# Layer-norm statistics one pair earlier, key-value sums taken tile by tile, num and den in separate PSUM banks: a linear-attention and Mish layer on one core

## The chip, the core and the metric

The kernel runs on one core of a Trainium2 chip. The metric is the device time of one execution in microseconds (us). The engines are TensorE (PE, its weight loads PEld), VectorE (DVE), ScalarE (ACT), GpSimd (POOL) and SyncE (SP). Each works through its own stream of instructions in order and waits for the others at semaphores.

## The reference, cut to what matters

`x` is 2048 x 448 in bf16. The result is `x` plus two branches that both read the layer norm of `x`: linear attention with 16 heads of 28, and a feed-forward part of width 1792 with Mish.

```python
xn = layernorm(x)                                   # per row, eps 1e-5
q, k, v = split_heads(xn @ wqkv)                    # H = 16, Dh = 28
phi_q = concat(softmax(q @ w_phi), softmax(-(q @ w_phi)))    # per head
phi_k = concat(softmax(k @ w_phi), softmax(-(k @ w_phi)))
kv, z = phi_k^T v, sum over s of phi_k              # per head, over all 2048 rows
A = ((phi_q kv) / (phi_q z + 1e-6)) @ wo
h = xn @ w1 + b1
B = (h * tanh(softplus(h))) @ w2
out = x + A + B
```

`kv` and `z` need all 2048 rows before any row of `A` can be finished. The feed-forward part needs only `xn`.

## The kernel before, in words

The 2048 rows are 16 tiles of 128; two tiles are a pair, so there are 8 pairs (`NP`). Everything stays in SBUF. `Prog.add` (L53) appends each operation to its engine's stream in the order of the Python code, and works out the semaphore waits from three lists of names: what it reads (`r`), writes (`w`) and which of the eight PSUM banks it uses (`x`). Any two engines that use the same bank are ordered. No planner reorders anything: the order of the code is the order on each engine.

**The loop over the pairs** (L491) is the first stage. `ln_a(j)` (L471) takes the statistics of a pair: two `bn_stats` (L251) and two `bn_aggr` (L254) on VectorE, then on GpSimd an add (L257) and a power of minus one half (L259) for `rstd`. `ln_b(j)` (L478) normalises its two tiles on VectorE (L263). `xT` transposes them on TensorE (L298) and ScalarE copies them out (L301). `vproj` (L310), `kproj` (L320) and, one pair behind, `qproj` (L347; a quarter of the rows and half of the heads each time) are 8 matmuls each. VectorE copies v out (`vevac`, L467), ScalarE takes both exponentials of k (`kexp`, L327, into a ring of four `Ek`) and of q (`qexp`, L354). Two pairs behind, `knorm` makes the softmax of k: a sum on VectorE (`Sk`, L333), its reciprocal (`rSk`, L335), and on GpSimd the multiplication that writes `phik` (L336). `masks()` (L239) puts five small operations on GpSimd in iteration 2. In iteration j the order is: `ln_a(j+2)`, `xT(j+1)`, `vproj(j)`, `vevac(j)`, `ln_b(j+2)`, `kproj(j)`, `kexp(j)`, `qproj` and `qexp` of j-1, `knorm(j-2)`. So on GpSimd `rstd` of pair j+2 stands behind the multiplication of `knorm(j-3)`, and on VectorE `ln_b(j+2)` stands ahead of the sum of `knorm(j-2)`.

**The up-projection** (L522) has 28 groups n: 8 matmuls (`ffn1_mm`, L418) into two of the banks 0 to 3, and one Mish on ScalarE (L432). Behind group 6 `kvz` (L358) runs 128 matmuls (L363) that sum `kv` and `z` over all tiles into banks 6 and 7, and VectorE masks them into `KVZ` (L370, L374). From group 7 on each group carries one row tile m: num and den by `nd_mm` (L381, four matmuls each for s = 1 into bank 7 and for s = 0 into bank 6), the division on VectorE (`nd`, L386, five operations L389 to L397) and GpSimd (L398), and three tiles behind the transposition of the attention rows (`oTr`, L405) in bank 4.

**The down-projection** (L536) gives every row tile 14 matmuls with W2 (L441) and 4 with Wo (L446) in one accumulation, an add of x on VectorE (L451) and a store.

Of the kernel before, what the change touches and what calls it, by code (L numbers as in the profile page):

```python
# [146 lines left out]
def ap_on(src, dims):  # L147
    return bass.AP(tensor=src.tensor, offset=src.offset, ap=[list(src.ap[0])] + [list(d) for d in dims])
# [9 lines left out]
def _kernel(es, nc, x2, A_wqkv, A_w_phi, A_wo, B_w1, B_b1, B_w2, out2):  # L158
    KC, KP, QG = 4, 112, 4
    E1 = DH + 1  # L160
    E2 = DH + 2
    pr = Prog(nc, es)
    pe = lambda fn, **k: pr.add("PE", fn, **k)
# [7 lines left out]
    def sb(name, shape, dtype=BF16):  # L171
        return es.enter_context(nc.sbuf_tensor(name, shape, dtype))
# [3 lines left out]
    mask = sb("mask", [KP, QG, E1], FP32)  # L176
# [25 lines left out]
    phik = hm[1].rearrange("p a b -> p (a b)").rearrange("p (t f) -> p t f", t=NT)  # L202
    rq = [sb(f"rq{i}", [P, 2, H], FP32) for i in range(2)]
    t1 = [sb(f"t1_{i}", [P, H, E1], FP32) for i in range(2)]
    t2 = [sb(f"t2_{i}", [P, H, E1], FP32) for i in range(2)]
# [5 lines left out]
    PS = es.enter_context(nc.psum_tensor("PS", [P, 8, 512], FP32))  # L211
# [38 lines left out]
    def ln_stats(t):  # L250
        dve(lambda v: v.bn_stats(stats[:, t, :], x_all[:, t, :]), r=[f"x{t}"], w=[f"st{t}"])  # L251

    def ln_aggr(t):
        dve(lambda v: v.bn_aggr(mv[:, t, :], stats[:, t, :]), r=[f"st{t}"], w=[f"mv{t}"])  # L254
# [7 lines left out]
    def ln_norm(t, eng):  # L262
        eng(lambda v: v.tensor_scalar(xn[t % NXN][:, :], x_all[:, t, :], mv[:, t, 0:1], rstd[:, t:t + 1],  # L263
                                      op0=ALU.subtract, op1=ALU.mult),
            r=[f"x{t}", f"mv{t}", f"rs{t}"], w=[f"xn{t % NXN}"])
# [76 lines left out]
    def qproj(tc, gp):  # L342
        for u in range(2):
            g = 2 * gp + u
            def f(e, g=g, u=u):
                for c in range(KC):
                    i = e.matmul(PS[0:KP, 6 + u, :], Wp[:, 0, c, g * KP:(g + 1) * KP],  # L347
                                 xnT[:, c, tc * 512:(tc + 1) * 512], start=(c == 0), stop=(c == KC - 1))
                return i
            pe(f, r=[f"xT{2 * tc}", f"xT{2 * tc + 1}", "Wp0"], x=[6 + u])  # L350

    def qexp(tc, gp):
        for s in range(2):
            act(lambda a, s=s: a.activation(EqT[:, s, 2 * gp:2 * gp + 2, tc * 512:(tc + 1) * 512],  # L354
                                            PS[0:KP, 6:8, :], ACT.Exp, scale=(1.0 if s == 0 else -1.0)),
                w=[f"Eq{tc}{gp}{s}"], x=[6, 7])

    def kvz():  # L358
        for s in range(2):
            def f(e, s=s):  # L360
                for g in range(QG):
                    for t in range(NT):
                        i = e.matmul(PS[0:KP, 6 + s, g * QG * E1:(g + 1) * QG * E1],  # L363
                                     phik[:, t, s * D + g * KP:s * D + (g + 1) * KP],
                                     v_ext[:, t, 4 * g:4 * g + 4, :], start=(t == 0), stop=(t == NT - 1))
                return i
            pe(f, r=[f"phik{j}" for j in range(8)] + [f"v{j}" for j in range(8)] + ["v1"], x=[6 + s])
            mk = ap_on(mask[:, 0, 0:1], [[0, QG], [E1, QG], [1, E1]])
            ps = PS[0:KP, 6 + s, 0:QG * QG * E1].rearrange("p (g j c) -> p g j c", g=QG, j=QG)
            dve(lambda v, s=s, mk=mk, ps=ps: v.tensor_tensor(KVZ[:, s, :, :, 0:E1], ps, mk, ALU.mult),  # L370
                r=["mask"], w=[f"KVZa{s}"], x=[6 + s])
            if s == 0:
                mz = ap_on(mask[:, 0, DH:E1], [[0, QG], [E1, QG], [1, 1]])
                dve(lambda v, mz=mz, ps=ps: v.scalar_tensor_tensor(KVZ[:, 0, :, :, DH:E1], ps[:, :, :, DH:E1],  # L374
                                                                   DEN_EPS, mz, op0=ALU.add, op1=ALU.mult),
                    r=["mask"], w=["KVZa0"], x=[6])

    def nd_mm(t, s):
            def f(e):
                for g in range(QG):  # L380
                    i = e.matmul(PS[:, 6 + s, g * QG * E2:(g + 1) * QG * E2], EqT[:, s, g, t * P:(t + 1) * P],  # L381
                                 KVZ[:, s, g, :, :], start=True, stop=True)
                return i
            pe(f, r=[f"Eq{t // 4}{gp}{s}" for gp in range(2)] + [f"KVZa{s}", "KVZ1"], x=[6 + s])

    def nd(t):  # L386
        i = t % 2
        nds = [PS[:, 6 + s, 0:H * E2].rearrange("p (h c) -> p h c", c=E2) for s in range(2)]
        dve(lambda v: v.reciprocal(rq[i][:, 1, :], nds[1][:, :, E1]), w=[f"rq{i}"], x=[7])  # L389
        dve(lambda v: v.tensor_tensor(rq[i][:, 0, :], nds[0][:, :, E1], rq[i][:, 1, :], ALU.mult),  # L390
            r=[f"rq{i}"], w=[f"rho{i}"], x=[6])
        dve(lambda v: v.tensor_tensor(t2[i][:, :, :], nds[1][:, :, 0:E1],  # L392
                                      ap_on(rq[i][:, 0, 0:1], [[1, H], [0, E1]]), ALU.mult),
            r=[f"rho{i}"], w=[f"t2{i}"], x=[7])
        dve(lambda v: v.tensor_tensor(t1[i][:, :, :], nds[0][:, :, 0:E1], t2[i][:, :, :], ALU.add),
            r=[f"t2{i}"], w=[f"t1{i}"], x=[6])
        dve(lambda v: v.reciprocal(rden[i][:, :], t1[i][:, :, DH]), r=[f"t1{i}"], w=[f"rd{i}"])  # L397
        pool(lambda g: g.tensor_tensor(o_sb[t % NO][:, :].rearrange("p (h d) -> p h d", d=DH), t1[i][:, :, 0:DH],  # L398
                                       ap_on(rden[i][:, 0:1], [[1, H], [0, DH]]), ALU.mult),
             r=[f"t1{i}", f"rd{i}"], w=[f"o{t % NO}"])  # L400
# [11 lines left out]
    def ffn1_mm(n, u):  # L412
        tcp, fc = n // FC, n % FC
        b = 2 * (n % 2)
        def f(e):
            for c in range(KC):
                o = tcp * 1024 + u * 512
                i = e.matmul(PS[:, b + u, :], W1[:, c, fc * P:(fc + 1) * P], xnT[:, c, o:o + 512],  # L418
                             start=(c == 0), stop=(c == KC - 1))
            return i  # L420
        pe(f, r=["W1"] + [f"xT{4 * tcp + 2 * u}", f"xT{4 * tcp + 2 * u + 1}"], x=[b + u])

    def mish(n):
        tcp, fc = n // FC, n % FC
        b = 2 * (n % 2)
        if tcp:
            rr = [f"phik{j}" for j in range(8)]
        elif fc < 7:
            rr = [f"WT{w}{h}" for w in range(2) for h in range(2)]
        else:  # L430
            rr = [f"Ek{i}{u}" for i in range(4) for u in range(2)]
        act(lambda a: a.activation(hm[tcp][:, fc, :].rearrange("p (u n) -> p u n", u=2), PS[:, b:b + 2, :], ACT.Mish,  # L432
                                   bias=b1T[:, fc:fc + 1]), r=["b1T"], w=[f"hm{tcp}"] + rr, x=[b, b + 1])
# [21 lines left out]
    NP = NT // 2  # L455
# [32 lines left out]
    w_mm(1, 0)  # L488
    w_mm(1, 1)
    ln_b(1)  # L490
    for j in range(NP):  # L491
        if j + 2 < NP:
            ln_a(j + 2)
        if j + 1 < NP:
            xT(j + 1)
        vproj(j)
        vevac(j)
        if j + 2 < NP:
            ln_b(j + 2)
        if j == 0:  # L500
            w_trans(0, 0)
            w_trans(0, 1)
        kproj(j)
        kexp(j)
        if j == 0:
            w_mm(0, 0)
            w_mm(0, 1)
        if j >= 1:
            qproj((j - 1) // 2, (j - 1) % 2)
            qexp((j - 1) // 2, (j - 1) % 2)  # L510
        if j >= 2:
            knorm(j - 2)
        if j == 2:
            masks()
            pe(lambda e: e.transpose(PSb[:, 3, 0:FC], b1_rows[0:FC, :], ident[0:FC, 0:FC]), r=["b1r", "ident"], x=[3])
            dve(lambda v: v.tensor_copy(b1T[:], PSb[:, 3, 0:FC]), w=["b1T"], x=[3])
    qproj(3, 1)
    qexp(3, 1)
    knorm(NP - 2)
    knorm(NP - 1)  # L520
    KV_AT = 6
    for n in range(2 * FC):  # L522
        m = n - KV_AT - 1
        ffn1_mm(n, 0)
        if 0 <= m < NT:
            nd_mm(m, 1)
        ffn1_mm(n, 1)
        mish(n)
        if 0 <= m < NT:
            nd_mm(m, 0)  # L530
            nd(m)
        if n == KV_AT:
            kvz()
        if 0 <= m - 3 < NT:
            oTr(m - 3)
# [31 lines left out]
```

## Time and profile before

| what | value |
|---|---|
| median of 3 runs | 201.37 us (201.27 to 204.5) |
| the profiled execution | 200.96 us, of which the traced span 199.0 us |
| mean granted TensorE clock | 0.983 |
| TensorE matmul busy | 176.7 us, 89% |
| VectorE busy | 84.4 us, 42% |
| ScalarE busy | 85.4 us, 43% |
| GpSimd busy | 51.7 us, 26% |

The span runs from the first to the last instruction; the remaining 1.96 us of the profiled execution lie around it. The matmul share is an average over stages, and matmuls waiting in the pipe count as busy. The stages are to be read one by one: the loop over pairs ends at about 67 us of the span, the up-projection runs to 141.57 us, and the down-projection fills the rest.

### The profile page before, as it was taken

How to read it: one execution, taken by the hardware profiler on the slowest of the kernel's cores; microseconds unless marked ns; L12 is line 12 of the kernel's file. 1: busy time of each engine (PE TensorE's matmuls, PEld its weight loads, DVE VectorE, ACT ScalarE, POOL GpSimd, SP SyncE). 2: the span in 40 equal slices, each digit the busy share in tenths (PEclk: the TensorE clock that was granted, in tenths of full speed). 3: DMA queues.
4: the chain of work that ended last, by engine and by line, in shares of the span. 5: the costliest groups of instructions: out<-in, count | busy, mean ns of one | idle time of the engine just before them, and what ended most of it. 6: DMA issues, size and time to landing. Idle time of an engine off the chain costs nothing.

```text
span 199.0 us, 2766 instructions
## 1 busy us (share of the span) xinstructions
PE 176.7 (89%) x1153; PEld 97.9 (49%) x1153; DVE 84.4 (42%) x172; ACT 85.4 (43%) x94; POOL 51.7 (26%) x54
## 2 busy tenths in 40 slices
PE   0579599959959598999999999999999999999994
PEld 0455455434535243487455555554455555555551
DVE  1535057565968950003777777770021211212121
ACT  2553768854767738640456666678500000000000
POOL 3310110838439795000233333331000000000000
PEclk9999999979999969999999999999999999999999
DMA  6999900000000000000000000000001010100101
GB/s 161 296 320 292 276 1 0 0 3 2 0 0 0 0 0 3 2 0 3 0 0 3 0 0 3 0 2 3 0 23 46 23 49 23 41 28 23 49 23 46
DMA packets 7556, 8.69 MB, mean 44 GB/s; under 512 B 952, under 2 KB 6840, under 8 KB 7544
## 3 DMA queue, kind: packets, MB, share of 16 engines
q1 hardware_dynamic: 6544, 8.09, 13.8%
q10 hardware_dynamic: 968, 0.43, 0.8%
q8 instruction: 9, 0.15, 0.3%
q14 instruction: 3, 0.02, 0.0%
q0 software_dynamic: 32, 0.00, 0.0%
HBM read 6.68 MB, written 1.84 MB: 43 GB/s over the span
## 4 chain that ended last, share of the span: by engine, by line
PE 72%; POOL 7%; DVE 7%; ACT 6%; DMA 4%; issue 1%; ACTq 0%; DVEq 0%; POOLq 0%
PE PS L418 21%; PE PS L441 21%; PE PS L446 6%; POOL hm L336 5%; PE PS L310 5%; PE PS L381 4%; DMA Wbd<-in_A_w_phi_dram 4%; PE PS L347 4%; PE PS L363 3%; PE PS L320 3%; DVE Sk L333 3%; ACT EqT L354 2%; PE PS L405 2%; ACT hm L327 2%; PE PS L284 1%; PE PS L298 1%
## 5 line engine op out<-in xcount | busy, mean ns | idle before, releaser
L418 PE MATMUL PS<-xnT,W 112*128 112x512 bf16 x224 | 54.7, 379 | 0.9 <-ACT hm L432 0.9
L441 PE MATMUL PS<-W,hm 128*128 128x448 bf16 x224 | 45.0, 353 | 0.0
L432 ACT ACTIVATE hm<-PS,b1T 128x1024 bf16<-128x1024 f32 x28 | 31.2, 1114 | 27.7 <-PE PS L418 27.6
L451 DVE TENSOR_TENSOR out_sb<-PS,x_all 128x448 bf16<-128x448 f32 x16 | 10.0, 625 | 53.0 <-PE PS L446 53.0
L441 PEld LDWEIGHTS PS<-W,hm 128*128 128x128 bf16 x224 | 21.9, 98 | 20.6
L336 POOL TENSOR_TENSOR hm<-hm,rSk 128x1792 bf16<-128x1792 bf16 x8 | 25.6, 3209 | 16.9 <-DVE rSk L335 11.5
L418 PEld LDWEIGHTS PS<-xnT,W 112*128 112x128 bf16 x224 | 20.3, 98 | 19.5 <-ACT hm L432 1.4
L327 ACT ACTIVATE hm<-PS 128x896 bf16<-128x896 f32 x16 | 13.8, 914 | 12.0 <-PE PS L320 12.0
L347 PE MATMUL PS<-xnT,Wp 112*112 112x512 bf16 x64 | 16.8, 410 | 2.0 <-ACT EqT L354 2.0
L354 ACT ACTIVATE EqT<-PS 112x1024 bf16<-112x1024 f32 x16 | 15.5, 1021 | 3.7 <-PE PS L347 3.7
L310 PE MATMUL PS<-Wqkv,xnT 112*128 112x448 bf16 x64 | 16.3, 407 | 0.0
L333 DVE TENSOR_REDUCE Sk<-hm 128x64 f32<-128x1792 bf16 x8 | 16.0, 2000 | 0.0
L398 POOL TENSOR_TENSOR o_sb<-t_0,rden 128x448 bf16<-128x448 f32 x8 | 7.5, 941 | 30.3 <-DVE rden L397 30.3
L446 PE MATMUL PS<-Wo,EqT 112*128 112x448 bf16 x64 | 14.8, 352 | 0.0
L467 DVE CAST v_ext<-PS 128x896 bf16<-128x896 f32 x8 | 8.6, 1078 | 14.0 <-PE PS L310 14.0
L320 PE MATMUL PS<-Wp,xnT 112*128 112x448 bf16 x64 | 13.5, 353 | 0.4 <-ACT hm L277 0.4
L381 PEld LDWEIGHTS PS<-KVZ,EqT 112*128 112x128 bf16 x128 | 8.3, 98 | 11.0 <-DVE t_0 L392 3.8
L347 PEld LDWEIGHTS PS<-xnT,Wp 112*112 112x112 bf16 x64 | 8.7, 138 | 8.4 <-ACT EqT L354 2.5
L381 PE MATMUL PS<-KVZ,EqT 112*128 112x120 bf16 x128 | 12.1, 217 | 0.5 <-DVE t_1 L392 0.2
L251 DVE BATCH_NORM_STATS2 stats<-x_all 128x6 f32<-128x448 bf16 x16 | 9.1, 608 | 4.2 <-DMA x_all<-in_A_x_dram 4.2
L298 PE MATMUL PS<-ident,xn 128*112 128x128 bf16 x64 | 6.5, 257 | 4.8 <-DVE xn L263 4.8
L398 POOL TENSOR_TENSOR o_sb<-t_1,rden 128x448 bf16<-128x448 f32 x8 | 7.5, 941 | 12.2 <-DVE rden L397 12.2
(49 smaller groups left out, 146.1 us busy)
## 6 DMA issues: line engine op xcount, KB each, us to landing
W<-in_B_w_dram SPq DMA_DIRECT2D x2, 1568.0 KB, 17.4
out_dram<-out_sb SPq DMA_DIRECT2D x16, 112.0 KB, 1.7
x_all<-in_A_x_dram SPq DMA_DIRECT2D x1, 896.0 KB, 10.0
Wqkv<-in_A_wqkv_dram SPq DMA_DIRECT2D x2, 392.0 KB, 7.3
x_all<-in_A_x_dram SPq DMA_DIRECT2D x2, 224.0 KB, 4.3
x_all<-in_A_x_dram SPq DMA_DIRECT2D x1, 448.0 KB, 7.1
Wqkv<-in_A_wqkv_dram ACTq DMA_DIRECT2D x1, 392.0 KB, 4.9
Wo<-in_A_wo_dram SPq DMA_DIRECT2D x1, 392.0 KB, 21.2
```

The costliest lines, as they stand in the source:

```text
L310: i = e.matmul(PS[:, 2 + u, 0:D], xnT[:, c, t * P:(t + 1) * P], Wqkv[:, c, 2 * D:3 * D], start=(c == 0), stop=(c == KC - 1))
L320: i = e.matmul(PS[:, 4 + u, 0:D], xnT[:, c, t * P:(t + 1) * P], Wp[:, 1, c, :], start=(c == 0), stop=(c == KC - 1))
L327: act(lambda a, s=s: a.activation(Ek[j % 4][:, :, s, :], PS[:, 4:6, 0:D], ACT.Exp, scale=(1.0 if s == 0 else -1.0)), w=[f"Ek{j % 4}{s}"], ...
L333: dve(lambda v: v.tensor_reduce(Sk[b][:, :], Ek[q][:, :, :, :].rearrange("p t s (h f) -> p (t s h) f", f=DH), AX.X, ALU.add), r=[f"Ek{q}0" ...
L336: pool(lambda g: g.tensor_tensor(phik[:, 2 * j:2 * j + 2, :].rearrange("p t (k f) -> p (t k) f", f=DH), Ek[q][:, :, :, :].rearrange("p t s ...
L347: i = e.matmul(PS[0:KP, 6 + u, :], Wp[:, 0, c, g * KP:(g + 1) * KP], xnT[:, c, tc * 512:(tc + 1) * 512], start=(c == 0), stop=(c == KC - 1))
L354: act(lambda a, s=s: a.activation(EqT[:, s, 2 * gp:2 * gp + 2, tc * 512:(tc + 1) * 512], PS[0:KP, 6:8, :], ACT.Exp, scale=(1.0 if s == 0 e ...
L381: i = e.matmul(PS[:, 6 + s, g * QG * E2:(g + 1) * QG * E2], EqT[:, s, g, t * P:(t + 1) * P], KVZ[:, s, g, :, :], start=True, stop=True)
L418: i = e.matmul(PS[:, b + u, :], W1[:, c, fc * P:(fc + 1) * P], xnT[:, c, o:o + 512], start=(c == 0), stop=(c == KC - 1))
L432: act(lambda a: a.activation(hm[tcp][:, fc, :].rearrange("p (u n) -> p u n", u=2), PS[:, b:b + 2, :], ACT.Mish, bias=b1T[:, fc:fc + 1]), r ...
L441: i = e.matmul(PS[:, b, 0:D], hm[t // 8][:, fc, o:o + P], W2[:, fc, :], start=(fc == 0), stop=False)
L446: i = e.matmul(PS[:, b, 0:D], oT[:, c, t * P:(t + 1) * P], Wo[:, c, :], start=False, stop=(c == KC - 1))
```

## The change

Three things move; no arithmetic and no transfer is added or taken away.

1. `ln_a` is issued three pairs ahead in place of two; `ln_a(2)` stands before the loop. `ln_b` stays two ahead.
2. The 128 matmuls of `kvz` are cut into eight calls `kv_mm(j)`, of 16 matmuls for one pair each, that accumulate side by side in banks 4 and 5. The first four stand behind the last `qproj`, the others behind groups 0 to 3. Group 0 of the up-projection moves ahead of the last `qproj`. The masking (`kvz`) follows behind group 3, and row tile m = 0 is worked on in group 5 in place of 7.
3. `nd_mm` for s = 0 alternates between banks 5 and 6 and is issued first in its group; s = 1 keeps bank 7 and is issued behind both halves of the up-projection group.

```diff
+    def kv_mm(j):
+        def f(e):
+            for t in (2 * j, 2 * j + 1):
+                for s in range(2):
+                    for g in range(QG):
+                        i = e.matmul(PS[0:KP, 4 + s, g * QG * E1:(g + 1) * QG * E1],
+                                     phik[:, t, s * D + g * KP:s * D + (g + 1) * KP],
+                                     v_ext[:, t, 4 * g:4 * g + 4, :], start=(t == 0 and g == 0),
+                                     stop=(t == NT - 1), skip_group_check=True)
+            return i
+        pe(f, r=[f"phik{j}", f"v{j}", "v1"], x=[4, 5])
+
     def kvz():
         for s in range(2):
-            def f(e, s=s):
-                for g in range(QG):
-                    for t in range(NT):
-                        i = e.matmul(PS[0:KP, 6 + s, g * QG * E1:(g + 1) * QG * E1],
...
-            pe(f, r=[f"phik{j}" for j in range(8)] + [f"v{j}" for j in range(8)] + ["v1"], x=[6 + s])
...
+    def nd_bank(t, s):
+        return 7 if s else 5 + t % 2
...
     w_mm(1, 1)
     ln_b(1)
+    ln_a(2)
     for j in range(NP):
-        if j + 2 < NP:
-            ln_a(j + 2)
+        if j + 3 < NP:
+            ln_a(j + 3)
         if j + 1 < NP:
             xT(j + 1)
         vproj(j)
...
+    ffn1_mm(0, 0)
+    ffn1_mm(0, 1)
     qproj(3, 1)
     qexp(3, 1)
     knorm(NP - 2)
     knorm(NP - 1)
-    KV_AT = 6
+    KV_END = 3
+    for j in range(4):
+        kv_mm(j)
     for n in range(2 * FC):
-        m = n - KV_AT - 1
-        ffn1_mm(n, 0)
+        m = n - KV_END - 2
+        if n:
+            ffn1_mm(n, 0)
+        if 0 <= m < NT:
+            nd_mm(m, 0)
+        if n:
+            ffn1_mm(n, 1)
+        mish(n)
         if 0 <= m < NT:
             nd_mm(m, 1)
-        ffn1_mm(n, 1)
-        mish(n)
-        if 0 <= m < NT:
-            nd_mm(m, 0)
             nd(m)
-        if n == KV_AT:
+        if 4 + n < NP:
+            kv_mm(4 + n)
+        if n == KV_END:
             kvz()
         if 0 <= m - 3 < NT:
             oTr(m - 3)
```

## Rows read from the trace of the kernel before

**Rows 1.** Windows: length, busy us (count) of PE, PEld, DVE, ACT, POOL; clock; DMA.

```profile
39.47:45.60 6.13, 3.80 (x17) 2.02 (x17) 4.06 (x6) 3.15 (x4) 2.71 (x5) 0.72 0.01 4
54.90:62.40 7.50, 5.48 (x34) 3.24 (x34) 5.83 (x6) 4.67 (x6) 4.08 (x4) 1.00 0.00 0
69.27:72.88 3.61, 3.61 (x9) 1.74 (x10) 3.24 (x4) 0.01 (x1) 3.61 (x2) 0.53 0.00 0
86.09:92.70 6.61, 6.61 (x129) 6.55 (x128) 0.87 (x2) 1.11 (x1) 0.00 (x0) 1.00 0.01 2
102.31:132.00 29.69, 29.69 (x245) 16.16 (x243) 21.87 (x60) 19.26 (x25) 11.33 (x13) 1.00 0.00 1
```

**Rows 2.** Timeline, TensorE: start, length, line; count; idle before and releaser in brackets.

```profile
34.22 0.65 PE L298 MATMUL PS<-ident,xn 128*112 128x128 bf16 x8
...
41.95 1.01 PE L298 MATMUL PS<-ident,xn 128*112 128x128 bf16 x8 [2.33 <-DVE xn L263]
...
49.47 0.74 PE L298 MATMUL PS<-ident,xn 128*112 128x128 bf16 x8 [0.44 <-DVE xn L263]
...
56.99 0.74 PE L298 MATMUL PS<-ident,xn 128*112 128x128 bf16 x8 [2.02 <-DVE xn L263]
...
65.35 1.89 PE L347 MATMUL PS<-xnT,Wp 112*112 112x512 bf16 x8
...
69.27 3.57 PE L347 MATMUL PS<-xnT,Wp 112*112 112x512 bf16 x8 [2.03 <-ACT EqT L354]
```

**Rows 3.** Timeline, VectorE and GpSimd, iterations 4 and 5 of the loop.

```profile
41.50 0.70 DVE L263 TENSOR_SCALAR xn<-x_all,mv,rstd 128x448 bf16<-128x448 bf16 x2 [3.98 <-POOL rstd L259]
...
44.80 3.21 POOL L336 TENSOR_TENSOR hm<-hm,rSk 128x1792 bf16<-128x1792 bf16 x1 [3.33 <-DVE rSk L335]
...
49.02 0.70 DVE L263 TENSOR_SCALAR xn<-x_all,mv,rstd 128x448 bf16<-128x448 bf16 x2 [2.10 <-POOL rstd L259]
...
49.64 2.02 DVE L333 TENSOR_REDUCE Sk<-hm 128x64 f32<-128x1792 bf16 x1
...
51.69 0.55 DVE L335 RECIPROCAL rSk<-Sk 128x64 f32<-128x64 f32 x1
...
53.38 1.06 DVE L467 CAST v_ext<-PS 128x896 bf16<-128x896 f32 x1
```

**Rows 4.** Chain of waits, iteration 1 of the loop: start, length, engine, line.

```profile
23.77 0.45 PE PS L298 x8
24.22 1.51 PE PS L310 x8
25.73 1.51 PE PS L320 x8
27.25 1.73 PE PS L347 x8
```

**Rows 5.** Timeline, VectorE: its idle time in iteration 0.

```profile
17.07 1.09 DVE L467 CAST v_ext<-PS 128x896 bf16<-128x896 f32 x1 [5.25 <-PE PS L310]
```

**Rows 6.** Page, transfers: size, us from issue to landing.

```profile
x_all<-in_A_x_dram SPq DMA_DIRECT2D x1, 896.0 KB, 10.0
```

**Rows 7.** Chain of waits: the exponentials ahead of the last `qproj`.

```profile
67.34 1.89 ACT EqT L354 x2
```

**Rows 8.** Timeline, GpSimd: the last three multiplications.

```profile
67.72 9.54 POOL L336 TENSOR_TENSOR hm<-hm,rSk 128x1792 bf16<-128x1792 bf16 x3 [1.22 <-DVE rSk L335]
```

**Rows 9.** Chain of waits: one group with a row tile, and the first down-projection.

```profile
115.76 0.31 PE PS L381 x4
116.06 0.86 PE PS L418 x4
116.92 0.21 PE PS L381 x4
117.14 0.23 PE PS L405 x4
...
141.57 2.65 PE PS L441 x14
```

More of the change, by code (lines that the diff above doesn't have):

```diff
@@ L356, in qexp @@
                 w=[f"Eq{tc}{gp}{s}"], x=[6, 7])
+    def kv_mm(j):
[9 more added lines that the diff above has]
+        pe(f, r=[f"phik{j}", f"v{j}", "v1"], x=[4, 5])
     def kvz():
         for s in range(2):
-            def f(e, s=s):
-                for g in range(QG):
-                    for t in range(NT):
-                        i = e.matmul(PS[0:KP, 6 + s, g * QG * E1:(g + 1) * QG * E1],
-                                     phik[:, t, s * D + g * KP:s * D + (g + 1) * KP],
-                                     v_ext[:, t, 4 * g:4 * g + 4, :], start=(t == 0), stop=(t == NT - 1))
-                return i
-            pe(f, r=[f"phik{j}" for j in range(8)] + [f"v{j}" for j in range(8)] + ["v1"], x=[6 + s])
             mk = ap_on(mask[:, 0, 0:1], [[0, QG], [E1, QG], [1, E1]])
-            ps = PS[0:KP, 6 + s, 0:QG * QG * E1].rearrange("p (g j c) -> p g j c", g=QG, j=QG)
+            ps = PS[0:KP, 4 + s, 0:QG * QG * E1].rearrange("p (g j c) -> p g j c", g=QG, j=QG)
             dve(lambda v, s=s, mk=mk, ps=ps: v.tensor_tensor(KVZ[:, s, :, :, 0:E1], ps, mk, ALU.mult),
-                r=["mask"], w=[f"KVZa{s}"], x=[6 + s])
+                r=["mask"], w=[f"KVZa{s}"], x=[4 + s])
             if s == 0:
@@ L375, in kvz, with f @@
                                                                    DEN_EPS, mz, op0=ALU.add, op1=ALU.mult),
-                    r=["mask"], w=["KVZa0"], x=[6])
+                    r=["mask"], w=["KVZa0"], x=[4])
+    def nd_bank(t, s):
+        return 7 if s else 5 + t % 2
     def nd_mm(t, s):
[L379 to L384, printed above, removed]
+        b = nd_bank(t, s)
+        def f(e):
+            for g in range(QG):
+                i = e.matmul(PS[:, b, g * QG * E2:(g + 1) * QG * E2], EqT[:, s, g, t * P:(t + 1) * P],
+                             KVZ[:, s, g, :, :], start=True, stop=True)
+            return i
+        pe(f, r=[f"Eq{t // 4}{gp}{s}" for gp in range(2)] + [f"KVZa{s}", "KVZ1"], x=[b])
     def nd(t):
         i = t % 2
-        nds = [PS[:, 6 + s, 0:H * E2].rearrange("p (h c) -> p h c", c=E2) for s in range(2)]
+        nds = [PS[:, nd_bank(t, s), 0:H * E2].rearrange("p (h c) -> p h c", c=E2) for s in range(2)]
         dve(lambda v: v.reciprocal(rq[i][:, 1, :], nds[1][:, :, E1]), w=[f"rq{i}"], x=[7])
         dve(lambda v: v.tensor_tensor(rq[i][:, 0, :], nds[0][:, :, E1], rq[i][:, 1, :], ALU.mult),
-            r=[f"rq{i}"], w=[f"rho{i}"], x=[6])
+            r=[f"rq{i}"], w=[f"rho{i}"], x=[nd_bank(t, 0)])
         dve(lambda v: v.tensor_tensor(t2[i][:, :, :], nds[1][:, :, 0:E1],
@@ L395, in nd @@
         dve(lambda v: v.tensor_tensor(t1[i][:, :, :], nds[0][:, :, 0:E1], t2[i][:, :, :], ALU.add),
-            r=[f"t2{i}"], w=[f"t1{i}"], x=[6])
+            r=[f"t2{i}"], w=[f"t1{i}"], x=[nd_bank(t, 0)])
         dve(lambda v: v.reciprocal(rden[i][:, :], t1[i][:, :, DH]), r=[f"t1{i}"], w=[f"rd{i}"])
```

## The prediction

> **What bounds the kernel now.** I read the windows first, because 89% matmul time over the whole span hides where TensorE stands still. From 102.31 us to the end of that window TensorE is busy throughout at full clock [rows 1], and so it is in the down-projection behind 141.57 us, which the change doesn't touch. The loss lies earlier: in 39.47 to 45.60 TensorE works 3.80 of 6.13 us, at a mean granted clock of 0.72, and in 69.27 to 72.88 it is busy at 0.53 [rows 1]. [...]
>
> TensorE's timeline names the waits [rows 2]. In iterations 4, 5 and 6 `xT` waits 2.33, 0.44 and 2.02 us for a normalised tile, and the last `qproj` waits 2.03 us for ScalarE. Two of the four waits are followed by slow matmuls: that `qproj` takes 3.57 us in place of 1.73 [rows 2, 4].
>
> VectorE's and GpSimd's timeline tells why the tile is late [rows 3]. The normalisation waits 3.98 and 2.10 us for `rstd`. GpSimd comes to `rstd` only after the 3.21 us multiplication queued ahead of it, and this waits for the reciprocal of a sum that VectorE does only behind the previous normalisation. The ring has a period of 41.50 to 49.02, that is 7.5 us, and everybody keeps to it. TensorE alone needs 0.45 + 1.51 + 1.51 + 1.73 = 5.20 us for an iteration, as iteration 1 shows [rows 4].
>
> **Part 1, the statistics three pairs ahead.** For six pairs two `bn_stats` and two `bn_aggr` on VectorE and two small operations on GpSimd move one iteration earlier. `rstd(j+3)` still stands ahead of the multiplication of pair j-2, but it is now needed an iteration later: the normalisation no longer waits for a multiplication queued in the iteration before it. The ring is open, and an iteration costs what its busiest engine needs. VectorE's full iteration runs from 49.02 to the end of `vevac` at 54.44 [rows 3]: 5.42 us. In the changed kernel only iterations 2 to 4 carry statistics, normalisation and sum together, so the 0.22 us above TensorE's 5.20 can't add up to more than VectorE's slack, and I set it to nothing (bounds 0 to 0.7 us). GpSimd's 3.21 and the short `rstd` fit in 5.20. The first extra pair of statistics falls into VectorE's idle 5.25 us ahead of the first `vevac` [rows 5], at no cost. The statistics of pair 4 are now wanted at some 19 us; their x, whose transfer takes 10.0 us from its issue at the start [rows 6], is there. No transfer is moved; SP's queue stays as it is.
>
> Starts against starts: `xT` of iteration 3 stands at 34.22 and `qproj` of iteration 7 at 65.35 [rows 2], 31.13 us. Afterwards it is four iterations of 5.20 (3 to 6), then `vproj` and `kproj` of iteration 7, 1.51 each: 23.82. **Gain 7.3 us**, the slow clock of 39.47 to 45.60 in it. `qproj` then starts at 58.0.
>
> **Parts 2 and 3, from there to the down-projection.** Before: 65.35 to 141.57 [rows 2, 9], 76.22 us. After, in TensorE's order:
> - From this `qproj` to the start of the last one, 3.92 us (65.35 to 69.27) is set by ScalarE: the exponentials of k, then those of q, which start at 67.34 and take 1.89 [rows 7]. TensorE now fills it with 1.73 + 1.72 (group 0), so the wait shrinks from 2.03 to 0.47 us; the 3.92 stay. Idle 0.44 in iteration 5 left no slow matmuls behind [rows 2], so I take the last `qproj` at 1.73.
> - 27 more groups of 2 x 0.86 [rows 9]: 46.4 us.
> - The 128 small matmuls are as many as before: 6.61 us, all at full clock [rows 1]. In 16s they cost 0.83 each. Breaking the run: nothing, since four small matmuls between two runs of other shapes already take only 0.21 [rows 9], 52 ns each, like the 52 ns of the long run; upper bound 8 x 0.1 = 0.8 us, from 0.31 against 0.21.
> - num and den: 32 x 0.21 = 6.7 us. Today one of the two takes 0.31 [rows 9], as bank 7 is still being read when its turn comes. Under the change bank 7 comes last in the group and the other bank has two groups to come free. VectorE needs 21.87 / 12 = 1.8 us for a tile [rows 1], within a group of 2.36.
> - 16 transpositions of 0.23 [rows 9]: 3.7 us.
>
> The sum is 3.92 + 1.73 + 46.4 + 6.6 + 6.7 + 3.7 = 69.1 us, a **gain of 7.1 us**.
>
> Does `kv_mm` wait, with all of the up-projection queued behind it on TensorE? `phik` of the last pair: `vproj` of iteration 7 ends at 56.5, then `vevac` 1.06, sum 2.02, reciprocal 0.55 [rows 3], and three multiplications of 9.54 together [rows 8]: about 69.7. It is wanted at 61.95 + 1.73 + 5 x 0.83 + 3 x 1.72 + 2 x 0.83 = 74.6. Margin 4.9 us, cost nothing. The masking (two operations today 0.87 us [rows 1], the third no longer than these) has group 4 and half of group 5, 2.58 us, before num needs it. The first Mish must be done before group 2 takes its banks: it stands behind exponentials (1.89) and a table load, and TensorE has 4.1 us of `kv_mm`, group 1 and another `kv_mm` in between, which covers it.
>
> **The sum.** 7.3 + 7.1 = 14.4 us from the profiled execution's 200.96 is 186.6. That execution stands 0.2% below the median of 201.37, so I say **187**.
>
> **The price that no row shows.** In the trace every normalisation behind iteration 3 runs just after `rstd`, while GpSimd has nothing long in hand [rows 3]. After the change those of pairs 6 and 7 come at about 43 and 48 us, in the middle of a multiplication of 3.21. If they run beside it, the cost is 0. If they can't, they wait for its end: that of pair 1 would run 41.5 to 44.7 (behind the masks and `rstd`, which today let go at 41.50), against an `xT` due at 44.6, so the second tile comes 0.6 us late, or 1.4 with GpSimd's next `rstd` slipping in between; that of pair 2 starts later by as much, about 48.0 to 51.2, and `xT` comes 1.2 late again. 1.9 to 2.6 us together. I take 0, since GpSimd's multiplications keep their 3.2 us beside VectorE's sums [rows 8], and keep both ends.
>
> [...]
>
> **Rivals.**
> - *The wait comes back as a block* (0.25). The normalisation waits for the running multiplication in place of the queued one: 1.9 to 2.6 us more, 189.3 with the median's offset. Against it: only an order of execution unseen so far; for it: both pairs fall inside a multiplication by the times above.
> - *The clock falls once more* (0.08). A wait of 2.02 us left full clock (1.00 in 54.90 to 62.40 [rows 1]), waits of 2.33 and 2.03 did not. A fall costs 1.5 to 1.8 us (3.57 against 1.73 [rows 2, 4]). Alone 188.7; on top of the block 191.
> - *The change doesn't open the ring* (0.07). If the loop keeps 7.5 us an iteration, only the 7.1 us remain: 194. Against it: the order of issue, in which no multiplication stands between a statistic and its use in time.
> - *No change* (0.05): the ring stays and chopping the small matmuls eats most of the 7.1. It needs over 10 us to be lost at once; 0.8 is the most that rows give for chopping.
> - *Slower* (0.03): `kv_mm` blocks TensorE's queue for `phik`. Its place is the calls for pairs 5 to 7 between groups 1 and 4; the price is each microsecond that `phik` of pair 7 comes after 74.6. It is slower when that is past 74.6 + 14.4 = 89, and by over 2% past 93, that is when the five multiplications from pair 3 on take two and a half times their 3.21. They run at 3.2 beside VectorE today [rows 3, 8].
>
> **How the numbers follow.** The forecast has 0.52. Its own range is 185 (the waits at the bank and between stages shrink a little more) to 188.5 (0.7 of VectorE and 0.8 of chopping). With the block, and the clock on top, the range goes to 191.5; some 2 in 10 lie outside, in the three last rivals and the tails. A measurement of this kernel tells about 2% from no change (197.3 to 205.4): faster 0.52 + 0.25 + 0.08 + 0.07 = 0.92, within 0.05, slower 0.03.
>
> **What would show it.** In the changed profile `xT` starts about every 5.2 us up to iteration 7, with no wait for the normalisation, and the clock of 39 to 46 us is 1.00. If pairs 6 and 7 are blocked, the normalisation ends right after a multiplication, or is recorded much longer than 0.7 us for two. The last `qproj` takes 1.73 and waits under 0.6. `kv_mm` shows eight runs of 0.83 with no wait for GpSimd. A group with a row tile takes 2.36 in place of 2.47, and the first down-projection starts near 127. A period of 7.5 us in the loop, or a wait for `phik`, would make the prediction wrong.

## The result and the profile after

The changed kernel takes 189.47 us (median of 4) against 201.35 us: the ratio is 0.9404, 95% interval 0.9375 to 0.9434, so 5.7% to 6.3% less. Medians count every execution; the ratios leave out those in a slow state, like the 204.5 us of the kernel before. I had said 187, 185 to 191.5. The time lies in the range, and beside the rival in which "the wait comes back as a block" (189.3), not beside the likeliest case. Its profiled execution took 189.63 us, with a span of 187.7 us at a mean granted clock of 0.989.

The span falls apart at three starts on TensorE's timeline: `xT` of iteration 3, `qproj` of iteration 7, and the first down-projection.

| stretch | before | forecast | after |
|---|---|---|---|
| start to `xT` of iteration 3 | 34.22 | 34.22 | 35.15 |
| to `qproj` of iteration 7 | 31.13 | 23.82 | 25.52 |
| to the first down-projection | 76.06 | 69.1 | 69.41 |
| to the end of the span | 57.6 | 57.6 | 57.6 |

The third stretch is 0.31 us above what it was to be, the second lost 1.70 us of its gain, and the first became 0.93 us longer, though almost nothing in it was changed. The three add up to the 2.94 us that the span has above the forecast. The first down-projection, on the timeline of the kernel before:

```profile
141.41 2.81 PE L441 MATMUL PS<-W,hm 128*128 128x448 bf16 x14
```

TensorE's timeline of the changed kernel (start, length, line, count; idle time before it and its releaser in brackets) answers to [rows 2]; its last row is the first down-projection:

```profile
35.15 0.65 PE L298 MATMUL PS<-ident,xn 128*112 128x128 bf16 x8
...
40.40 0.61 PE L298 MATMUL PS<-ident,xn 128*112 128x128 bf16 x8
...
46.07 0.74 PE L298 MATMUL PS<-ident,xn 128*112 128x128 bf16 x8 [0.30 <-DVE xn L263]
...
52.31 0.74 PE L298 MATMUL PS<-ident,xn 128*112 128x128 bf16 x8 [0.75 <-DVE xn L263]
...
60.67 1.89 PE L347 MATMUL PS<-xnT,Wp 112*112 112x512 bf16 x8
...
64.58 1.93 PE L347 MATMUL PS<-xnT,Wp 112*112 112x512 bf16 x8 [0.30 <-ACT EqT L354]
66.35 4.34 PE L363 MATMUL PS<-v_ext,hm 128*112 128x116 bf16 x80
...
72.26 1.00 PE L363 MATMUL PS<-v_ext,hm 128*112 128x116 bf16 x16
...
77.39 1.00 PE L363 MATMUL PS<-v_ext,hm 128*112 128x116 bf16 x16
...
130.08 2.81 PE L449 MATMUL PS<-W,hm 128*128 128x448 bf16 x14
```

The starts of `xT` show the periods: 5.25 us, then 5.67 and 6.24. The ring of 7.5 us is open, but in two iterations `xT` still waits for a normalisation, 0.30 and 0.75 us. The last `qproj` waits 0.30 in place of 2.03 us and is fast, and no `kv_mm` waits for GpSimd.

Why the normalisation is late again is on VectorE's timeline, which answers to [rows 3]:

```profile
38.37 1.71 DVE L263 TENSOR_SCALAR xn<-x_all,mv,rstd 128x448 bf16<-128x448 bf16 x2
...
44.70 1.62 DVE L263 TENSOR_SCALAR xn<-x_all,mv,rstd 128x448 bf16<-128x448 bf16 x2
...
49.69 2.87 DVE L263 TENSOR_SCALAR xn<-x_all,mv,rstd 128x448 bf16<-128x448 bf16 x2
```

and on GpSimd's, over the same time:

```profile
36.21 3.21 POOL L336 TENSOR_TENSOR hm<-hm,rSk 128x1792 bf16<-128x1792 bf16 x1 [5.53 <-DVE b1T L525]
39.36 0.19 POOL L240 MEMSET mask<- 112x116 f32 x1
...
42.66 3.21 POOL L336 TENSOR_TENSOR hm<-hm,rSk 128x1792 bf16<-128x1792 bf16 x1 [0.23 <-DVE rSk L335]
...
48.91 3.21 POOL L336 TENSOR_TENSOR hm<-hm,rSk 128x1792 bf16<-128x1792 bf16 x1 [2.03 <-DVE rSk L335]
...
63.03 9.55 POOL L336 TENSOR_TENSOR hm<-hm,rSk 128x1792 bf16<-128x1792 bf16 x3 [1.22 <-DVE rSk L335]
```

Two normalisations took 0.70 us in [rows 3]; here they are recorded as 1.71, 1.62 and 2.87. No idle time stands before them: they are recorded as running all the while. Line L263's own view gives the longest single one, 2.56 us against a median of 0.39 (minimum, median, maximum in ns):

```profile
L263 DVE TENSOR_SCALAR xn<-x_all,mv,rstd x16: 383/392/2561, 6.8 to 52.2; 128x448 bf16<-128x448 bf16 x16
```

In each pair it is the first tile that is long:

```profile
38.37 1.31 DVE L263 TENSOR_SCALAR xn<-x_all,mv,rstd 128x448 bf16<-128x448 bf16 x1
...
44.70 1.31 DVE L263 TENSOR_SCALAR xn<-x_all,mv,rstd 128x448 bf16<-128x448 bf16 x1
...
49.69 2.56 DVE L263 TENSOR_SCALAR xn<-x_all,mv,rstd 128x448 bf16<-128x448 bf16 x1
```

Each ends 0.13 to 0.14 us behind an instruction of GpSimd: at 52.25 and 46.01 behind multiplications that end at 52.12 and 45.87, and at 39.68 behind a short memset that follows the multiplication and ends at 39.55. GpSimd's multiplication came first each time and keeps its 3.21 us; the normalisation, which came second, pays.

The longer start is the clock. The windows view (length, busy us of PE, PEld, DVE, ACT, POOL; clock; DMA) of the changed kernel has TensorE at 0.50 in iteration 1, behind a wait of 2.21 us for ScalarE:

```profile
23.50:26.60 3.10, 3.10 (x10) 1.20 (x9) 0.00 (x0) 1.40 (x2) 0.00 (x0) 0.50 0.32 76
```

The wait is there before the change too, 2.21 us, with no fall behind it: over the same 23.50 to 26.60 us the granted clock of the kernel before is 1.00. TensorE's timeline has two differences in this stretch, in the transposition of weights (L274) and in the first `vproj` behind the wait (L310). Before:

```profile
16.83 1.60 PE L274 MATMUL PS<-ident,Wqkv 112*112 112x112 bf16 x16
...
24.06 1.68 PE L310 MATMUL PS<-Wqkv,xnT 112*128 112x448 bf16 x8
```

and after:

```profile
16.47 0.99 PE L274 MATMUL PS<-ident,Wqkv 112*112 112x112 bf16 x16
...
23.37 3.19 PE L310 MATMUL PS<-Wqkv,xnT 112*128 112x448 bf16 x8
```

From `xT` to `qproj` of iteration 1 the fall costs 1.7 us (22.86 to 28.02, against 23.61 to 27.09), and 0.75 us of it had been won before, since `xT` starts that much earlier. The same transpositions are as fast (0.99 to 1.11 us) in the traces of three of the kernels below (the banks alone, and the two on the filling), and in all three the clock falls behind this wait; in the six others that have the wait they take 1.50 to 1.70 us, as before the change, and there it doesn't fall. So in these traces the clock falls here where the transpositions ahead of the wait had run in 0.99 to 1.11 us, and not where they had taken 1.50 to 1.70. Why they and the clock differ from one execution to another is open.

The four executions of the changed kernel have mean clocks of 0.989, 0.991, 1.000 and 0.991 and times of 189.63, 189.47, 188.77 and 189.46 us: the fall is a matter of the execution, and 0.7 to 0.9 us of the time go with it, less than the 1.7 of the fall alone.

### The profile page after: what moved, and what is told of

The parts are those of the page before. It is cut to its first block, busy times and chain, and to the rows that moved or that the text cites. A ratio compares the mean times of both kernels' runs of the same rounds, so it can differ in the third digit from the quotient of the medians.

```text
span 187.7 us, 2766 instructions
## 1 busy us (share of the span) xinstructions
PE 172.5 (92%) x1153; PEld 98.2 (52%) x1153; DVE 90.3 (48%) x172; ACT 85.0 (45%) x94; POOL 51.8 (28%) x54
## 4 chain that ended last, share of the span: by engine, by line
PE 78%; DVE 11%; ACT 4%; DMA 4%; issue 1%; ACTq 1%; POOL 0%; POOLq 0%; DVEq 0%
PE PS L426 25%; PE PS L449 23%; PE PS L454 6%; PE PS L310 6%; DMA Wbd<-in_A_w_phi_dram 4%; PE PS L389 4%; PE PS L363 4%; PE PS L320 3%; DVE xn L263 3%; DVE Sk L333 3%; PE PS L347 3%; DVE v_ext L475 2%; PE PS L413 2%; ACT hm L327 2%; PE PS L284 1%; PE PS L298 1%
## 5 line engine op out<-in xcount | busy, mean ns | idle before, releaser
L310 PE MATMUL PS<-Wqkv,xnT 112*128 112x448 bf16 x64 | 16.4, 408 | 0.0
L347 PE MATMUL PS<-xnT,Wp 112*112 112x512 bf16 x64 | 15.2, 380 | 0.3 <-ACT EqT L354 0.3
L389 PEld LDWEIGHTS PS<-KVZ,EqT 112*128 112x128 bf16 x128 | 9.6, 98 | 7.6
L347 PEld LDWEIGHTS PS<-xnT,Wp 112*112 112x112 bf16 x64 | 8.2, 130 | 6.0 <-ACT EqT L354 0.8
L263 DVE TENSOR_SCALAR xn<-x_all,mv,rstd 128x448 bf16<-128x448 bf16 x16 | 9.7, 646 | 2.3 <-POOL rstd L259 2.3
```

The lines of the kernel that those rows point to most:

```text
L310: i = e.matmul(PS[:, 2 + u, 0:D], xnT[:, c, t * P:(t + 1) * P], Wqkv[:, c, 2 * D:3 * D], start=(c == 0), stop=(c == KC - 1))
L389: i = e.matmul(PS[:, b, g * QG * E2:(g + 1) * QG * E2], EqT[:, s, g, t * P:(t + 1) * P], KVZ[:, s, g, :, :], start=True, stop=True)
```

## The experiments

**Which part gives what.** Three kernels carry a part of the change each. The first:

```diff
     ln_b(1)
+    ln_a(2)
     for j in range(NP):
-        if j + 2 < NP:
-            ln_a(j + 2)
+        if j + 3 < NP:
+            ln_a(j + 3)
```

> The kernel before with part 1 alone: statistics three pairs ahead. Theory (the ring of 7.5 us opens, but the normalisations of pairs 5 to 7 are blocked by the multiplication that runs beside them): the loop gains 7.3 us less 1.7 us of the block, 201.35 - 5.6 = 195.7 us; two normalisations take 1.6 to 2.9 us in iterations 3 to 5, and the last qproj still waits 2 us. Rival (the loop was not what gave the time; the up-projection was): under 2 us gained, 199.5 or more.

194.75 us, ratio 0.9615 (0.954 to 0.9691). Between `xT` of iteration 3 and `qproj` of iteration 7 it takes 25.50 us, as the changed kernel does, with the same waits. Its timeline on TensorE:

```profile
44.98 0.74 PE L298 MATMUL PS<-ident,xn 128*112 128x128 bf16 x8 [0.29 <-DVE xn L263]
...
51.23 0.74 PE L298 MATMUL PS<-ident,xn 128*112 128x128 bf16 x8 [0.75 <-DVE xn L263]
...
63.50 1.93 PE L347 MATMUL PS<-xnT,Wp 112*112 112x512 bf16 x8 [2.03 <-ACT EqT L354]
```

The loop gained 31.13 - 25.50 = 5.6 us and the rival falls. The last row is worth a look: the wait of 2.03 us is as long as in [rows 2], but here the `qproj` behind it runs at full speed, 1.93 in place of 3.57 us. (The median is above the profiled execution's 193.57 us, the only one of the four with a mean clock of 1.000.)

The second kernel is the changed one with `ln_a` two pairs ahead again, that is parts 2 and 3:

```diff
     ln_b(1)
-    ln_a(2)
     for j in range(NP):
-        if j + 3 < NP:
-            ln_a(j + 3)
+        if j + 2 < NP:
+            ln_a(j + 2)
```

> The changed kernel with the statistics two pairs ahead, as before. Theory: the loop keeps its period of 7.5 us, and what remains is the gain behind the loop, 76.22 - 69.6 = 6.6 us: 194.7 us. Its normalisations run alone again, 0.7 us for two. Rival (the two parts overlap, so that one alone gives nearly everything): 190 to 191 us. If the gains of this run and of the one with part 1 alone add up to 11.9 us, they are independent.

194.96 us, ratio 0.966 (0.9578 to 0.9742). Its loop stretch is 31.15 us, as before the change, with waits of `xT` of 2.34, 0.45 and 2.03 us; the stretch behind it is 69.42, as after. So the parts act in their own stretches. The two gains add up to 3.85% + 3.4% = 7.25%, more than the 5.96% of both; each of the two is uncertain by some 0.8%, and the profiles show two reasons: the stretch behind the loop also became 1.6 us shorter with part 1 alone (74.43 for 76.06), where the clock happened not to fall, which the filling of part 2 gives as well; and the changed kernel's start carries the 0.93 us.

The third has only the banks and the order of num and den:

```diff
+    def nd_bank(t, s):
+        return 7 if s else 5 + t % 2
...
         ffn1_mm(n, 0)
         if 0 <= m < NT:
-            nd_mm(m, 1)
+            nd_mm(m, 0)
         ffn1_mm(n, 1)
         mish(n)
         if 0 <= m < NT:
-            nd_mm(m, 0)
+            nd_mm(m, 1)
             nd(m)
```

> The kernel before with part 3 alone: num in banks 5 and 6 in turn and issued first in its group, den in bank 7 and issued last. Theory (16 groups lose 0.10 us each at the bank that is still being read, the first three some 0.3 us): 1.6 to 2.2 us gained, 199.3 us, a group of 2.37 in place of 2.47 us. Rival (the wait moves to bank 7): no gain, 201.3 us.

199.76 us, ratio 0.9872 (0.9799 to 0.9944): some 1.3% less, at the edge of what can be told from no change. The timeline is clearer than the time: the stretch behind `qproj` of iteration 7 is 73.59 us, 2.47 less than before, while the clock fell in iteration 1 of this execution (its first `vproj` behind the wait takes 2.92 us, against 1.68 in the kernel before) and made the start 1.38 us longer. A group, from one transposition to the next, takes 104.63 - 102.26 = 2.37 us, against 2.47 in [rows 9] (0.31 + 0.86 + 0.21 + 0.23 + 0.86):

```profile
102.26 0.39 PE L409 MATMUL PS<-ident,o_sb 128*112 128x128 bf16 x4
102.48 1.03 PE L422 MATMUL PS<-xnT,W 112*128 112x512 bf16 x4
103.35 0.37 PE L385 MATMUL PS<-KVZ,EqT 112*128 112x120 bf16 x4
103.56 1.03 PE L422 MATMUL PS<-xnT,W 112*128 112x512 bf16 x4
104.42 0.37 PE L385 MATMUL PS<-KVZ,EqT 112*128 112x120 bf16 x4
104.63 0.39 PE L409 MATMUL PS<-ident,o_sb 128*112 128x128 bf16 x4
```

**What fills the gap ahead of the last `qproj`.** Two kernels take the filling apart. One is the changed kernel with group 0 back in the loop:

```diff
-    ffn1_mm(0, 0)
-    ffn1_mm(0, 1)
     qproj(3, 1)
...
-        if n:
-            ffn1_mm(n, 0)
+        ffn1_mm(n, 0)
```

> The changed kernel with group 0 of the up-projection behind the last qproj and the first four kv_mm, not ahead of it. Theory (ScalarE sets the start of the last qproj, and group 0 only fills its 2 us): the wait of 2.03 us comes back whole, the first Mish comes later and group 2 waits for it; 1.7 us more, 191.2 us, with up to 1.7 us on top where the clock falls behind the wait. Rival (the order here is indifferent, since the same work must be done): 189.5 us.

The ratio to the kernel before is 0.9525 (0.9432 to 0.9619), and all four executions take longer than the changed kernel: 193.12, 193.47 and 193.78 us at mean clocks of 0.981 and 0.982, and 190.29 at 0.991. In the traced one, of 193.12, the stretch behind `qproj` of iteration 7 is 72.72 us, 3.31 more: the wait and the clock (0.83 granted in 60 to 70 us), both. The execution at 0.991, the mean clock that the changed kernel has too, is only 0.8 us above it, where I had expected 1.7 for the wait alone; it wasn't traced.

```profile
64.75 3.51 PE L347 MATMUL PS<-xnT,Wp 112*112 112x512 bf16 x8 [2.03 <-ACT EqT L354]
68.09 3.51 PE L363 MATMUL PS<-v_ext,hm 128*112 128x116 bf16 x64
```

The other is the kernel before with group 0 moved ahead, and nothing else:

```diff
+    ffn1_mm(0, 0)
+    ffn1_mm(0, 1)
     qproj(3, 1)
...
-        ffn1_mm(n, 0)
+        if n:
+            ffn1_mm(n, 0)
...
```

> The kernel before with group 0 of the up-projection ahead of the last qproj, and nothing else; the 128 small matmuls stay behind group 6. Theory (the wait of 2.03 us is filled, but without kv_mm behind the last qproj group 2 then waits 2.7 us for the first Mish in place of 0.94): nothing gained by the order, 1.6 us by the clock where the last qproj now runs at full speed: 199.7 to 201.4 us. Rival (filling the wait is the whole gain of this stretch, 3.4 us): 198 us.

202.43 us, ratio 1.0046 (1.0022 to 1.0069): no gain, half a per cent the other way, and above my range. The stretch behind `qproj` of iteration 7 is 76.11 us, against 76.06; what the traced execution lost more lies in its start, where the clock fell in iteration 1 (3.11 us for the `vproj` behind the wait, against 1.68). The order gives nothing, as expected, but the clock isn't saved either; the fall moves with the wait:

```profile
70.73 1.93 PE L347 MATMUL PS<-xnT,Wp 112*112 112x512 bf16 x8 [0.30 <-ACT EqT L354]
72.51 1.89 PE L418 MATMUL PS<-xnT,W 112*128 112x512 bf16 x8
77.11 10.49 PE L418 MATMUL PS<-xnT,W 112*128 112x512 bf16 x40 [2.72 <-ACT hm L432]
```

The last `qproj` is fast now; but group 2 waits 2.72 us for the first Mish, and the 40 matmuls behind that take 10.49 us, at a granted clock of 0.80 in 80 to 85 us, in place of the 8.81 that they take in the kernel with part 1 alone:

```profile
69.88 8.81 PE L418 MATMUL PS<-xnT,W 112*128 112x512 bf16 x40 [0.99 <-ACT hm L432]
```

Only with `kv_mm` as work behind the last `qproj` does the filling pay. That is what cutting the 128 matmuls is worth here: they are movable work, not cheaper work.

**What blocks the normalisation.** First an attempt that changed nothing:

```diff
-        eng(lambda v: v.tensor_scalar(xn[t % NXN][:, :], x_all[:, t, :],
+        eng(lambda v: v.tensor_scalar(xn[t % NXN][:, :].rearrange("p (a b) -> p a b", a=7),
+                                      x_all[:, t, :].rearrange("p (a b) -> p a b", a=64),
                                       mv[:, t, 0:1], rstd[:, t:t + 1],
```

> The changed kernel with the normalisation's access patterns written as 7 x 64 on the output and 64 x 7 on the input, the same elements in the same order, so that the tile doesn't split into equal halves on both sides. [...] Rival (anything that VectorE reads from SBUF as bf16 is held up): two normalisations still take 1.6 to 2.9 us, 189.5 us. Rival 2 (the other pattern makes every normalisation slower by more than the block cost): 190 us or more.

189.65 us, and the profile still has 128x448 on both sides: the instruction that ran has the form of the changed kernel's. It tells nothing of what blocks the normalisation and is one more run of the changed kernel; its profiled execution ran at a clock of 1.000, with a loop stretch of 25.51 and 188.58 us.

Next, the multiplication in four pieces:

```diff
-        pool(lambda g: g.tensor_tensor(
-            phik[:, 2 * j:2 * j + 2, :].rearrange("p t (k f) -> p (t k) f", f=DH),
...
+        for u in range(2):
+            for s in range(2):
+                pool(lambda g, u=u, s=s: g.tensor_tensor(
+                    phik[:, 2 * j + u, s * D:(s + 1) * D].rearrange("p (h f) -> p h f", f=DH),
+                    Ek[q][:, u, s, :].rearrange("p (h f) -> p h f", f=DH),
...
```

> The changed kernel with each multiplication on GpSimd cut into four pieces of a quarter (one tile and one sign each), nothing else. Theory (the normalisation is blocked until the instruction then running on GpSimd ends): it now waits for one piece of some 0.85 us at most, two normalisations take 0.7 to 1.6 us in place of 1.6 to 2.9, the 0.75 us wait of xT in iteration 5 goes, and the time from xT of iteration 3 to qproj of iteration 7 is 24.0 us in place of 25.5; 188.0 us. Rival (GpSimd's traffic slows VectorE whatever the length of an instruction): normalisations as before, 25.5 us and 189.5 us.

189.13 us, ratio to the kernel before 0.9383 (0.9342 to 0.9425). The profiled execution, at 187.89 us and a clock of 0.999, has a loop stretch of 24.56 us: 0.96 us shorter, where I had expected 1.5. The median hardly differs from the changed kernel's: the other executions took 189.06 to 189.26 us at a mean clock of 0.991, 0.2 to 0.4 less than the changed kernel's at 0.991; the traced one is 0.9 below the changed kernel's at 1.000. So the times alone don't tell the theory from its rival; the trace does. VectorE's timeline of the traced one:

```profile
37.81 2.10 DVE L263 TENSOR_SCALAR xn<-x_all,mv,rstd 128x448 bf16<-128x448 bf16 x2
...
44.53 1.31 DVE L263 TENSOR_SCALAR xn<-x_all,mv,rstd 128x448 bf16<-128x448 bf16 x2
...
49.22 1.31 DVE L263 TENSOR_SCALAR xn<-x_all,mv,rstd 128x448 bf16<-128x448 bf16 x2
```

and GpSimd's beside the last of them:

```profile
48.44 4.00 POOL L338 TENSOR_TENSOR hm<-hm,rSk 128x448 bf16<-128x448 bf16 x4 [0.73 <-DVE rSk L335]
```

The pair that had taken 2.87 us takes 1.31: the wait is as long as a piece, not as the whole. Its second tile ends at 50.53, 0.14 us behind the piece that ran beside it:

```profile
49.45 0.94 POOL L338 TENSOR_TENSOR hm<-hm,rSk 128x448 bf16<-128x448 bf16 x1
...
49.52 1.01 DVE L263 TENSOR_SCALAR xn<-x_all,mv,rstd 128x448 bf16<-128x448 bf16 x1
```

So the length of GpSimd's instruction sets it, and the rival falls. That of 38 us got longer (2.10 in place of 1.71), which I hadn't counted on: it ends at 39.91, 0.13 us behind a memset of GpSimd that ends at 39.78, as if each of its two tiles had been held by an instruction of its own; in iteration 5 a second tile still keeps `xT` waiting, for 0.47 us; and four pieces cost GpSimd 4.00 in place of 3.21 us. One piece of the 32 is longer than the rest (minimum, median, maximum in ns):

```profile
L338 POOL TENSOR_TENSOR hm<-hm,rSk x32: 938/940/1057, 35.6 to 72.5; 128x448 bf16<-128x448 bf16 x32
```

It is the one that starts at 44.65, inside a normalisation that runs from 44.53 to 44.91, and it cost GpSimd 0.12 us. The piece at 49.45 starts inside a normalisation too (49.22 to 49.60) and isn't longer. So the traces show the normalisation waiting; of GpSimd waiting in its turn they show little.

Then the same tile by another instruction of VectorE:

```diff
+    xacc = sb("xacc", [P, NT], FP32)
...
-    op0=ALU.subtract, op1=ALU.mult),
+    op0=ALU.subtract, op1=ALU.mult, accum_out=xacc[:, t:t + 1]),
```

> The changed kernel with a normalisation that also writes a reduction of its output to a spare column, which nobody reads. [...] Rival (every VectorE instruction that reads and writes SBUF is blocked): two still take over 1.6 us in iterations 3 to 5.

In this form `xn` doesn't hold the normalised tile. What is read and waited for is the same, and so is what is written but for the spare column. 188.57 us, ratio to the kernel before 0.9387 (0.9342 to 0.9433). GpSimd's timeline has a multiplication from 42.11 to 45.32:

```profile
42.11 3.21 POOL L337 TENSOR_TENSOR hm<-hm,rSk 128x1792 bf16<-128x1792 bf16 x1
```

and VectorE's two normalisations inside it:

```profile
44.06 0.73 DVE L264 TENSOR_SCALAR_CACHE_REDUCE xn<-x_all,mv,rstd 128x448 bf16<-128x448 bf16 x1
...
44.71 0.73 DVE L264 TENSOR_SCALAR_CACHE_REDUCE xn<-x_all,mv,rstd 128x448 bf16<-128x448 bf16 x1
```

It is nearly twice as long alone (0.73 against 0.39 us), and as long in the middle of a multiplication. TensorE's timeline shows no idle time for a tile, though the `xT` of 45.13 us takes 0.81 in place of 0.61; the loop stretch is 24.61 us, with 0.35 us of it a wait for another operation (the bias column, L526). So not every VectorE instruction that reads and writes SBUF is blocked: the form that takes 0.39 us alone is, the one of 0.73 us isn't. Why the one and not the other, no run here shows.

**A version that beats both.** If the block is a matter of what runs beside what, the order can avoid it: VectorE normalises between the sum and the reciprocal of the softmax, while GpSimd must wait for that reciprocal. To have the time for it, the normalisation goes three pairs ahead as well:

```diff
-    def knorm(j):
+    def knorm(j, mid=None):
...
+        if mid is not None:
+            ln_b(mid)
         dve(lambda v: v.reciprocal(rSk[b][:, :], Sk[b][:, :]), r=[f"Sk{b}"], w=[f"rSk{b}"])
...
+    ln_b(2)
     for j in range(NP):
...
-        if j + 2 < NP:
-            ln_b(j + 2)
+        if j < 2:
+            ln_b(j + 3)
...
-            knorm(j - 2)
+            knorm(j - 2, j + 3 if j + 3 < NP else None)
-        if j == 2:
+        if j == 0:
             masks()
```

> The changed kernel with the normalisation three pairs ahead as well, issued on VectorE between the sum and the reciprocal of the softmax of k, that is while GpSimd has to wait for the reciprocal; the masks move to iteration 0. Nothing is computed differently. Theory (the block is a matter of what runs beside what): two normalisations take 0.7 us everywhere, xT waits for none, and the time from xT of iteration 3 to qproj of iteration 7 falls from 25.5 to 23.9 us: 187.9 us. Rival (VectorE's work per iteration is what holds the loop): 25 us or more for this stretch, 189.5 us.

187.52 us (187.32 to 187.58), ratio to the kernel before 0.9309 (0.9279 to 0.9339). The loop stretch is 58.43 - 34.54 = 23.89 us, the normalisations take 0.70 us for two again, and `xT` waits nowhere:

```profile
34.54 0.65 PE L298 MATMUL PS<-ident,xn 128*112 128x128 bf16 x8
...
44.99 0.61 PE L298 MATMUL PS<-ident,xn 128*112 128x128 bf16 x8
...
50.20 0.61 PE L298 MATMUL PS<-ident,xn 128*112 128x128 bf16 x8
...
58.43 1.89 PE L349 MATMUL PS<-xnT,Wp 112*112 112x512 bf16 x8
```

Line L263's own view has no long one left:

```profile
L263 DVE TENSOR_SCALAR xn<-x_all,mv,rstd x16: 386/391/397, 7.1 to 45.5; 128x448 bf16<-128x448 bf16 x16
```

The last run takes the 2.2 us wait of iteration 0 as well, by putting other work in it:

```diff
         vproj(j)
         vevac(j)
+        if j == 1:
+            w_mm(0, 1)
...
         if j == 0:
             w_mm(0, 0)
-            w_mm(0, 1)
```

> The version with the normalisation between sum and reciprocal, and the second half of the query weights' product behind vproj of pair 1 in place of ahead of xT, so that TensorE no longer stands 2.2 us for ScalarE's copy in iteration 0. Theory (that wait is on the path, and it is the one behind which the clock falls in some executions): 1.5 to 2.2 us less than the version before it, 186 us, with a granted clock of 0.99 or more in 19 to 30 us in every execution. Rival (ScalarE's chain of copies sets this stretch, whatever TensorE does meanwhile): the wait moves to kproj or qproj of iteration 1, under 0.5 us gained.

184.89 us, ratio to the kernel before 0.9176 (0.9143 to 0.9208), 2.6 us below the version before it and more than expected. The profiled execution has a clock of 1.000, and the wait for ScalarE's copy is 0.25 us:

```profile
22.80 0.62 PE L284 MATMUL PS<-Wbd,hm 112*112 112x112 bf16 x8 [0.25 <-ACT Wp L288]
```

The start is 31.91 us in place of the 34.54 of the version before it. Of these 2.63 us, 1.96 are the wait; the rest stands ahead of it, where the weights' transpositions take 1.11 in place of 1.61 us; behind the wait of 0.25 us in place of 2.21 the clock didn't fall.

## Why the prediction was right, and where its likeliest case was not

- *The ring opens*: right. Part 1 alone took 5.6 us off the loop, and the waits for `rstd` are gone from iterations 3 to 5.
- *An iteration costs TensorE's 5.20 us, VectorE's 5.42 add nothing*: right. With no block the stretch is 23.89 us against the 23.82 of the sum.
- *"I take 0" for the normalisations beside a multiplication*: wrong, and this is the step that failed. It costs 25.52 - 23.89 = 1.6 us by the version that avoids it (there the masks move and the normalisation is a pair earlier too), 1.3 by the run with the accumulator (25.52 - 24.61, and the 0.35 of its own wait), and 1.5 by the two long periods of the changed kernel (5.67 and 6.24 against 5.20); I had 1.9 to 2.6 for the other end. The reason I gave, that multiplications keep 3.2 us beside VectorE's sums [rows 8], was about another instruction, and about the wrong one of the two: the multiplication keeps its 3.21 us beside the normalisation too, and it is the normalisation that waits, 2.56 us for a tile in place of 0.39. Both normalisations that I had named were caught, and a third, of pair 5, whose delay TensorE doesn't see. The rival was described as it happened and had half the forecast's chance; the times in the sum put both pairs inside a multiplication, so it should have had the larger one. That the time came out so near its 189.3 is in part luck: the block cost less than the rival said, and the clock in the start, which is not in the rival, made up for it.
- *Behind the loop*: right, 69.41 us against 69.1. The gain is 6.65 us and not 7.1, in part because my 76.22 took its start from the timeline and its end from the chain of waits; on the timeline alone it is 76.06. The pieces are as summed: 0.84 us for a later `kv_mm` (72.26 to the next group's start at 73.10), 0.30 us of wait in place of 0.47, no wait for `phik`. The last multiplication ends at 72.58 (63.03 and 9.55) and is wanted at 77.39, so the margin for `phik` is 4.8 us, against my 4.9; no run made it smaller. The two runs on the filling show that its first two pieces work only together.
- *The clock*: I had it fall once more with 0.08, in the loop. It fell in iteration 1 of the traced execution (0.50 in 23.50 to 26.60 us), on a stretch where TensorE's work is the same as before, and by their mean clocks, 0.991 each, in two of the other three. The sum was 186.6 for a profiled execution, which took 189.63: of the 3.0 us between, 1.70 are the loop, 0.93 the start and 0.31 the stretch behind the loop.

## What to carry to other kernels

When a change lets an instruction run at a new time, list what will be running on the other engines at that time; a wait in a queue may have hidden that the two get in each other's way, as the waits for `rstd` did here. A normalisation recorded at 2.56 us where its like take 0.39, with no idle time before it, and ending 0.13 us behind another engine's instruction, pointed to a block and not to slow work; the cure was another order (0.70 us for two again), and it was free because GpSimd had a wait of its own, 1.28 us for the reciprocal. Work that filled a gap of 2.03 us paid nothing (202.43 us) while the next wait behind it, 2.72 us, stayed open; with `kv_mm` as work there it paid (a ratio of 0.9404 to the kernel before, against 0.9525 without the filling).

## What the runs showed of the hardware

- A bf16 normalisation of 128 x 448 on VectorE takes 0.39 us alone and up to 2.56 us beside a GpSimd multiplication that started first and itself stays at 3.21 us; it ends 0.13 to 0.14 us behind it. The form with an accumulator takes 0.73 us in both cases.
- TensorE's granted clock fell behind a wait of 2.03 us in three kernels (3.57, 3.51 and 3.30 us for a `qproj`; granted 0.53 in 69.27 to 72.88 us of the kernel before) and not in a fourth (1.93 us). Behind the 2.21 us wait of iteration 0 it fell (to 0.50 in 23.50 to 26.60 us of the changed kernel) in the four traces in which the transpositions ahead of it had run in 0.99 to 1.11 us, and not in the seven in which they had taken 1.50 to 1.70. A price for it in a sum is a chance and not a term.
- Four GpSimd multiplications of 448 columns take 4.00 us where one of 1792 takes 3.21. Of 32 of them one took 1.06 us in place of 0.94, one that started inside a normalisation; another that did so took 0.94.
